# A Mamba-2 scan and a low-rank mixer in one kernel: fills from a repeated column of ones, and a longer fill before the first C B^T

## The chip, the cores and the metric

The kernel runs on one core of a Trainium2 chip. The metric is the device time of one execution in microseconds; lower is better. The engines named below are TensorE (matmul; PE in the profile, its weight loads PEld), VectorE (DVE), ScalarE (ACT), GpSimd (POOL) and SyncE (SP), which issues every load and store.

## The reference

Two blocks follow one another. The first is a chunked state-space scan over x (4 batches, 8 heads, 768 steps, 32 channels) with decays `a` and matrices B and C of 16 columns; the second is a mixer with a low-rank product over the sequence and a two-layer network over the channels.

```python
for c in range(nc):                       # chunks of 32 steps
    cum = np.cumsum(log_a[:, :, sl], axis=-1)
    L = np.exp(cum[:, :, :, None] - cum[:, :, None, :]) * causal
    M = np.einsum('bhin,bhjn->bhij', Cc, Bc) * L
    y_intra = np.einsum('bhij,bhjd->bhid', M, xc)
    y_inter = np.einsum('bhin,bhnd->bhid', Cc, state) * np.exp(cum)[:, :, :, None]
    y[:, :, sl] = y_intra + y_inter
    state = decay_full * state + (decay_from_j * Bc, xc summed over j)
# y as (4, 768, 256)
h = y.transpose(0, 2, 1) @ U @ V
u = y + h.transpose(0, 2, 1)
out = u + np.maximum(u @ w_ch1, 0.0) @ w_ch2
```

## The kernel before

The scan is done in 12 pairs of 128-step blocks (3 pairs for each of 4 batches). For a pair k the steps are: `Q` or `P` scales pieces of B and C by the decays on VectorE (tile `BC`); `V` or `T` transposes them on TensorE (L480) and copies them out (tiles `T` and `Cm`); `g` forms C B^T (L511); `m` and `M` mask it on VectorE; `s` and `u` form and carry the state (L543); `n` and `i`, `j` form the output inside and between chunks (L635, L613); `y` copies it out, `t` turns it. The mixer's steps (`p`, `q`, `a`, `S`, `f`, `e`, `h`, `d`, `U`) follow batch by batch; their matmuls are those of L725, and they make most of the time.

The order of all work is written out by hand. `LOADS` names the first loads; `PLAN` is a string of words, each a step with its indices, and every engine gets its instructions in the order in which `follow` (L859) meets the words. The words `b`, `x`, `w`, `W`, `Z`, `z` issue loads, all on SyncE's queue. The plan begins (L37):

```python
'x1.1 F2.0 A0 Q0.1 x1.0 Q0.0 b2.2 A1 F2.1 Q0.2 V0.1.1 V0.0.0 K0 F1.3 Q1.2 Q1.1 g0 m0 Q1.0 s0 '
```

The word `F` calls `warm` (L320), which calls `idle` (L133): a **fill**, a matmul into a PSUM bank whose result nobody reads. `F2.1` is a fill of two times 128 columns into a bank of tag `x`; the second index chooses among the tags `w`, `x`, `z`, `y`. Two more fills stand in the code ahead of the plan: `warm(3, "x")` (L325), the first work of TensorE, and `warm(1, "x")` (L331), behind the transposes of the decays (L330). Each fp32 matmul is two weight loads and two matmul instructions in the trace. A fill takes `ident` as weights, and `ident` once, two or three times side by side as moving operand.

Before the plan VectorE and GpSimd make the constants. VectorE begins with `ones` (L291) and `ref` (L306); GpSimd makes `ident` (by `make_identity`, L289) and then the triangles `upto` and `low` out of `ones`. `ident` is also what the transposes need. The decays: `a_sb` is loaded (L171), transposed (L330), clipped on VectorE, put through the logarithm on ScalarE (L336); `A0` and `A1` (L366, L370) make the factors `F` of it, `K0` (L381, L384) the carried decays. Between `K0` and `g0` stands the fill `F1.3`; `g0` needs the tiles `Cm`, whose last part ScalarE writes (L490).

VectorE's instructions all show L159 in the profile, the line of a helper; they are told apart by their tiles. Loads show L185, fills L138.

Of the kernel before, what the change touches and what calls it, by code (L numbers as in the profile page):

```python
# [10 lines left out]
FP32 = mybir.dt.float32  # L11
# [22 lines left out]
LOADS = (  # L34
    'b0.0 b0.1 b0.2 x0.0 x0.1 b1.0 b1.1 b1.2 ')
PLAN = (
# [40 lines left out]
def kernel(  # L77
# [27 lines left out]
    nc = tc.nc  # L105
    P = 128
# [17 lines left out]
    const = ctx.enter_context(tc.tile_pool(name="const", bufs=1))  # L124
# [8 lines left out]
    def idle(t, n):  # L133

        while n > 0:
            m = min(n, max(t.shape[1] // P, 1), 4)
            w = min(P, t.shape[1])
            nc.tensor.matmul(out=t[:, :m * w].rearrange("p (m i) -> p m i", i=w), lhsT=ident,  # L138
                             rhs=ident[:, None, :w].to_broadcast([P, m, w]), start=True, stop=True)
            n -= m  # L140

    def bank(tag, *dims):
# [5 lines left out]
    class Kept:  # L148
# [15 lines left out]
    vector = Kept(nc.vector)  # L164
# [7 lines left out]
        out=a_sb,  # L172
# [112 lines left out]
    for word in LOADS.split():  # L285
        loads[word[0]](*(int(v) for v in word[1:].split(".")))

    ident = const.tile([P, P], FP32)
    make_identity(nc, ident)  # L289
    ones = const.tile([P, P], FP32)  # L290
# [29 lines left out]
    def warm(n, tag="w"):  # L320

        idle(bank(tag, 4 * P), n)
# [6 lines left out]
    for g in range(2):  # L329
# [3 lines left out]
        out=la.rearrange("p b c h -> p b h c"),  # L333
# [575 lines left out]
```

## Time and profile before

| what | value |
|---|---|
| median of 3 runs | 226.42 us (226.41, 226.42, 228.46) |
| span of the profiled execution, first to last instruction | 224.7 us |
| its own time around the span | not given by the page |
| TensorE busy | 216.0 us (96%) |
| VectorE, ScalarE, GpSimd busy | 156.7, 114.3, 14.3 us |
| DMA | 14.56 MB in 69518 packets, 63792 of them under 512 bytes |
| first fill | starts at 1.43 us |
| fill ahead of the first C B^T | starts at 8.53 us, lasts 0.38 us |
| first C B^T | starts at 9.56 us |

Times in rows of the profile count from the first instruction. A row of the timeline is: start, duration, engine, line, operation, the tile written and those read, the shape, the count, and in brackets how long the engine stood idle before it and what ended that. A row of a table of stretches is: the stretch, its length, the busy time of each engine with the number of instructions, the clock granted to TensorE, the mean busy share of the DMA engines, GB/s. In a group of instructions the number behind the busy time is the mean duration of one in nanoseconds.

### The profile page before, as it was taken

Reading aid. Unit: us, or ns where it says so; the run is one execution under the profiler, and the core shown is the slowest. Engines: PE = TensorE matmul, PEld = TensorE weight load, DVE = VectorE, ACT = ScalarE, POOL = GpSimd, SP = SyncE. Lnnn points to the kernel's source line nnn. Section 1 sums busy time; section 2 is a strip of 40 time slices with the busy share of each in tenths; the row PEclk is TensorE's granted clock in tenths of the full one; section 3 lists DMA queues with packets and bytes.
Section 4 is the critical chain, followed back from the end, with each engine's and each line's share of the span. In section 5 each row is a group of like instructions: output and inputs, shape, how many; then the busy total and the mean of one; then the engine's idle time right before and its main releaser. Section 6 shows DMA issues by size and latency. Waiting matters only on the chain.

```text
span 224.7 us, 7010 instructions
## 1 busy us (share of the span) xinstructions
PE 216.0 (96%) x3012; PEld 182.8 (81%) x3012; DVE 156.7 (70%) x329; ACT 114.3 (51%) x261; POOL 14.3 (6%) x37
## 2 busy tenths in 40 slices
PE   7888989999999999999999999999999999999993
PEld 4656655656668898987999898887998999999993
DVE  4776878899998866969717785758437964764921
ACT  3334946856994346334453632475237545655410
POOL 3021010012100000202101000100000000000000
PEclk9999999999999999999999999999999999999999
DMA  6997799788645203600002602000020000100011
GB/s 88 127 111 144 132 130 287 139 163 230 92 65 72 51 23 59 84 23 26 3 26 48 96 0 73 3 3 3 1 71 1 0 0 26 47 0 28 32 38 47
DMA packets 69518, 14.56 MB, mean 65 GB/s; under 512 B 63792, under 2 KB 67696, under 8 KB 69488
## 3 DMA queue, kind: packets, MB, share of 16 engines
q1 hardware_dynamic: 69488, 14.13, 34.6%
q8 instruction: 23, 0.38, 0.7%
q14 instruction: 7, 0.06, 0.1%
HBM read 10.98 MB, written 3.15 MB: 63 GB/s over the span
## 4 chain that ended last, share of the span: by engine, by line
PE 91%; DVE 2%; DMA 2%; SPq 1%; issue 1%; POOL 0%; ACT 0%; POOLq 0%; DVEq 0%
PE x L725 31%; PE z L725 24%; PE y L725 12%; PE y L613 4%; PE y L635 3%; PE w L480 3%; PE x L511 3%; PE w L656 2%; DMA bc<-in_B_dram 2%; PE w L543 2%; PE z L511 2%; PE x L138 1%; SPq L185 1%; PE w L679 1%; PE w L138 1%
## 5 line engine op out<-in xcount | busy, mean ns | idle before, releaser
L159 DVE SCALAR_TENSOR_TENSOR words<-words 128x768 fp32r<-128x768 f32 (+6 forms) x44 | 34.6, 806 | 1.9 <-ACT words L416 0.6
L725 PE MATMUL z<-u,w 128*128 128x384 f32 x144 | 34.0, 350 | 0.0
L725 PE MATMUL x<-u,w 128*128 128x384 f32 x144 | 33.1, 348 | 0.0
L730 ACT ACTIVATE x<-x 128x384 f32<-128x384 f32 (+1 forms) x30 | 13.6, 452 | 25.3 <-PE x L725 25.1
L725 PEld LDWEIGHTS z<-u,w 128*128 128x128 f32 x144 | 24.5, 188 | 1.3 <-DVE words L159 0.2
L725 PEld LDWEIGHTS x<-u,w 128*128 128x128 f32 x144 | 24.0, 188 | 1.3 <-ACT x L730 0.6
L159 DVE SCALAR_TENSOR_TENSOR words<-x,words 128x384 fp32r<-128x384 f32 x24 | 13.2, 555 | 16.4 <-ACT words L759 13.7
L725 PE MATMUL x<-w2c,words 128*128 128x256 f32 x112 | 22.5, 338 | 0.0
L730 ACT ACTIVATE z<-z 128x384 f32<-128x384 f32 (+1 forms) x27 | 12.5, 463 | 14.1 <-PE z L725 13.6
L725 PEld LDWEIGHTS x<-w2c,words 128*128 128x128 f32 x112 | 18.2, 189 | 1.3
L725 PE MATMUL y<-w,words 128*128 128x256 f32 x144 | 19.1, 282 | 0.0
L725 PEld LDWEIGHTS y<-w,words 128*128 128x128 f32 x144 | 18.5, 188 | 0.3 <-DVE ytok L159 0.3
L159 DVE SCALAR_TENSOR_TENSOR words<-z,words 128x384 fp32r<-128x384 f32 x24 | 13.2, 551 | 5.7 <-ACT words L759 5.7
L759 ACT ACTIVATE words<-x 128x384 fp32r<-128x384 f32 x24 | 11.6, 490 | 6.3 <-PE x L725 6.1
L759 ACT ACTIVATE words<-z 128x384 fp32r<-128x384 f32 x24 | 11.6, 491 | 4.9 <-PE z L725 4.8
L648 ACT COPY yT<-y 128x256 f32<-128x256 f32 x24 | 7.8, 384 | 10.9 <-PE y L613 10.7
L569 POOL TENSOR_TENSOR Sm<-S,own 128x256 f32<-128x256 f32 (+1 forms) x12 | 7.7, 644 | 87.5 <-DVE S L159 58.1
L159 DVE SCALAR_TENSOR_TENSOR S<-S,kept,w 128x64 f32<-128x64 f32 x40 | 11.2, 280 | 2.7 <-PE w L543 0.9
L613 PE MATMUL y<-T,Sm 32*64 32x64 f32 x352 | 12.4, 239 | 0.4 <-POOL Sm L569 0.3
L725 PE MATMUL x<-w,words 128*128 128x256 f32 x96 | 12.6, 282 | 0.0
L725 PEld LDWEIGHTS x<-w,words 128*128 128x128 f32 x96 | 12.0, 188 | 0.1
L511 PE MATMUL x<-Cm,T 32*64 32x128 f32 x192 | 11.0, 307 | 1.0 <-ACT Cm L490 0.7
(152 smaller groups left out, 400.5 us busy)
## 6 DMA issues: line engine op xcount, KB each, us to landing
words<-in_moe_w_ch_dram SPq DMA_DIRECT2D x7, 512.0 KB, 6.1
x<-in_x_dram SPq DMA_DIRECT2D x24, 128.0 KB, 3.7
out_dram<-ytok SPq DMA_DIRECT2D x24, 128.0 KB, 1.7
bc<-in_B_dram SPq DMA_DIRECT2D x24, 64.0 KB, 3.7
bc<-in_C_dram SPq DMA_DIRECT2D x12, 128.0 KB, 3.8
words<-in_moe_w_ch_dram SPq DMA_DIRECT2D x2, 256.0 KB, 4.5
words<-in_moe_V_dram SPq DMA_DIRECT2D x4, 48.0 KB, 3.1
words<-in_moe_U_dram SPq DMA_DIRECT2D x1, 192.0 KB, 3.5
```

Source lines behind the costliest of these rows:

```text
L138: nc.tensor.matmul(out=t[:, :m * w].rearrange("p (m i) -> p m i", i=w), lhsT=ident, rhs=ident[:, None, :w].to_broadcast([P, m, w]), start= ...
L159: self.last = call(*args, **kwargs)
L480: nc.tensor.transpose(out=tp[:, i, v], in_=s["BC"][:, i, c + v].rearrange("p h n -> p (h n)"), identity=ident)
L511: nc.tensor.matmul(out=g[r][cols, c], lhsT=s["T"][rows, 0, c, cols], rhs=s["Cm"][rows, :, :, ts(2 * c + p, Q)].rearrange("r v t i -> r v i ...
L543: nc.tensor.matmul(out=s["A"][p][ts(r, Q), v], lhsT=s["BC"][half, 0, v, 2 * r:2 * r + 2].rearrange("p h n -> p (h n)"), rhs=x_sb[k][half, ...
L569: nc.gpsimd.tensor_tensor(out=s["Sm"][:, sl], in0=s["S"][:, sl].rearrange("p i (s d) -> p i s d", s=2), in1=own2[:, b, 4 * q + sl.start:4 ...
L613: product = nc.tensor.matmul(out=y[p][ts(r % 2, H), r // 2, c], lhsT=own[ts(r, Q)], rhs=s["T"][ts(r, Q), 1, :, ts(2 * c + p, Q)].rearrange ...
L635: product = nc.tensor.matmul(out=y[p][ts(i, Q), n, c], lhsT=x_sb[k][half, c, h], rhs=s["M"][half, h // 2, c, h % 2], start=fresh(k, p, [i] ...
L648: nc.scalar.copy(out=yp[:, :, :, p], in_=st[k]["y"][p])
L725: nc.tensor.matmul(out=t, lhsT=lhsT, rhs=rhs, start=start, stop=True, skip_group_check=True)
L730: nc.scalar.activation(t, t, AF.Copy, scale=1.0 + EPS)
L759: nc.scalar.activation(gs[j, m // 2][0][:, m % 2], t, AF.Relu, scale=NEAR)
```

## The change

A tile `one` of one column is added and set to 1.0 on VectorE, ahead of `make_identity` and of `ones`. The fills read it in place of `ident`: the weights are that column repeated 128 times, the moving operand is that column repeated over all columns of the fill. In the plan `F1.3` becomes `F3.3`: the fill between `K0` and `g0` has 384 columns in place of 128, in the same bank.

```diff
-    ... A1 F2.1 Q0.2 V0.1.1 V0.0.0 K0 F1.3 Q1.2 Q1.1 g0 m0 Q1.0 s0 '
+    ... A1 F2.1 Q0.2 V0.1.1 V0.0.0 K0 F3.3 Q1.2 Q1.1 g0 m0 Q1.0 s0 '
@@ def idle(t, n):
-            nc.tensor.matmul(out=t[:, :m * w].rearrange("p (m i) -> p m i", i=w), lhsT=ident,
-                             rhs=ident[:, None, :w].to_broadcast([P, m, w]), start=True, stop=True)
+            nc.tensor.matmul(out=t[:, :m * w].rearrange("p (m i) -> p m i", i=w), 
+                             lhsT=one.to_broadcast([P, P]),
+                             rhs=one[:, None, :].to_broadcast([P, m, w]), start=True, stop=True)
@@
+    one = const.tile([P, 1], FP32)
+    vector.memset(one, 1.0)
     ident = const.tile([P, P], FP32)
     make_identity(nc, ident)
     ones = const.tile([P, P], FP32)
```

2 rows, old and new, of the table PLAN are left out of this document.

## The prediction

> **What bounds the kernel now.** I read the page's first two parts, then a table by stretches, then the waits of VectorE and TensorE in the first 33 us, because every edit lies there. The page first (busy shares; the span in 40 slices of 5.6 us):
>
> ```profile
> span 224.7 us, 7010 instructions
> PE 216.0 (96%) x3012; PEld 182.8 (81%) x3012; DVE 156.7 (70%) x329; ACT 114.3 (51%) x261; POOL 14.3 (6%) x37
> PE   7888989999999999999999999999999999999993
> DMA  6997799788645203600002602000020000100011
> ```
>
> TensorE is the bound of the whole, but the first six slices show it mostly at 70 to 90% beside DMA engines that are 60 to 90% busy. The table by stretches says it sharper (columns: stretch: length, busy PE, PEld, DVE, ACT, POOL, PEclk, DMA share, GB/s):
>
> ```profile
> 0.00:10.00 10.00, 7.92 (x56) 5.49 (x64) 5.13 (x20) 3.67 (x9) 2.06 (x12) 1.00 0.85 106
> 10.00:21.00 11.00, 9.95 (x374) 6.71 (x358) 7.73 (x26) 3.84 (x14) 2.01 (x5) 1.00 1.04 126
> 21.00:33.00 12.00, 10.49 (x307) 6.99 (x308) 9.75 (x30) 8.28 (x23) 1.49 (x4) 1.00 0.87 129
> 33.00:60.00 27.00, 26.62 (x419) 16.31 (x425) 24.77 (x57) 19.60 (x43) 2.68 (x4) 1.00 0.82 187
> 60.00:225.00 165.00, 161.05 (x1890) 147.34 (x1881) 109.35 (x200) 78.87 (x176) 6.07 (x12) 1.00 0.16 34
> ```
>
> Up to 33 us the DMA engines are as good as full (shares 0.85, 1.04, 0.87) and TensorE idles 2.08, 1.05 and 1.51 us; from there on it idles 0.38 us in 27 and 3.95 in 165. So the time is the moment at which the DMA-fed start hands over to TensorE, plus some 192 us that no edit touches. Which wait ends last in the start? The timeline's rows for VectorE and TensorE carry it in brackets (idle before, and what ended it):
>
> ```profile
> 6.14 1.02 DVE L159 TENSOR_TENSOR BC<-bc,F 128x128 f32<-128x128 f32 x3 [1.44 <-DMA bc<-in_B_dram]
> ...
> 20.21 0.69 DVE L159 TENSOR_TENSOR BC<-bc,F 128x512 f32<-128x512 f32 x1 [1.26 <-DMA bc<-in_C_dram]
> ```
>
> ```profile
> 21.55 0.63 PE L480 MATMUL w<-ident,BC 128*128 128x128 f32 x4 [0.67 <-DVE S L159]
> ...
> 32.65 0.66 PE L480 MATMUL w<-ident,BC 128*128 128x128 f32 x4 [0.40 <-DVE BC L159]
> ```
>
> VectorE stands idle until a piece of B or C has landed, and TensorE stands behind it at 21.55 (through the `S` that VectorE makes after 20.21) and at 32.65. The chain that ended last shows the second joint, where a landing of B is followed (over VectorE) by TensorE, which holds the chain from there:
>
> ```profile
> 28.00 3.78 DMA bc<-in_B_dram
> ...
> 32.65 0.66 PE w L480 x4
> ```
>
> What TensorE gains before 21.55 is given back at these joints as longer idle time; what it loses is paid only beyond 0.67 us at 21.55, and again beyond 0.40 us at 32.65. The landings themselves should not move: SyncE issues its loads one behind the other from 0.81 us on, and the first of them that takes over a buffer in use is this one, after 24 us:
>
> ```profile
> 0.81 0.38 SPq L171 DMA_DIRECT2D a_sb<-in_a_dram  x1
> ...
> 24.17 1.28 SPq L185 DMA_DIRECT2D x<-in_x_dram  x1
> ```
>
> **Part one: the column of ones.** The timeline's rows by engine: VectorE's first memset and, for its price, the memset of one column for `bias`; GpSimd's `ident`, and `upto` behind it; then TensorE:
>
> ```profile
> 0.90 0.17 DVE L159 MEMSET ones<- 128x128 f32 x1 [0.90 <-PEq L893]
> ...
> 4.34 0.06 DVE L159 MEMSET bias<- 128x1 f32 x1
> ```
>
> ```profile
> 1.08 0.29 POOL masks.py:199 TENSOR_SCALAR_AFFINE_SELECT ident<-ident 128x128 f32<-128x128 f32 x1
> 1.33 0.29 POOL L294 TENSOR_SCALAR_AFFINE_SELECT upto<-ones 128x128 f32<-128x128 f32 x1
> ```
>
> ```profile
> 1.43 1.65 PE L138 MATMUL x<-ident 128*128 128x384 f32 x2 [1.43 <-POOL ident masks.py:199]
> ...
> 2.88 0.29 PEld L330 LDWEIGHTS w<-ident,a_sb 96*128 96x128 f32 x2 [0.95 <-DMA a_sb<-in_a_dram]
> ```
>
> Added: one memset of 0.06 us, ahead of `ones` on VectorE. It would run 0.90 to 0.96; with the 0.06 us that lay between the end of `ident` (1.08 + 0.29 = 1.37) and the first fill (1.43), the fill starts at about 1.02, **0.41 us sooner**. `ones` and what follows it move back by 0.06 us or less; `upto`, which reads `ones`, starts at 1.33 behind `ident` on POOL while `ones` ends at 1.07, so 0.2 us of cover remains. The first work that counts, the transposes of `a_sb`, waits for its DMA until 2.88 in either kernel. The fill ahead of them then ends at 1.02 + 1.65 = 2.67 instead of 3.08: the gain becomes idle time in front of 2.88. One wait is added: those transposes are now the first to need `ident`; it has been done since 1.37, so this costs at most one extra wait instruction, a few hundredths, and is covered by the VectorE wait that ends at 6.14. Worth: **0**.
>
> The later fills keep their number, their place and, but for one, their columns. No row here has a matmul whose operands repeat one column. Bounds: not quicker than the 128-column step below; if reading it were twice as slow, the fills of 384 and 256 columns that follow C B^T (0.82 and 0.60 us by the rows of part two; F2.1 and F3.0 before the first joint, F2.3 before the second) would each cost as much again: 0.60 + 0.82 - 0.67 = 0.75 us passes the first joint, 0.75 + 0.60 - 0.40 = 0.95 us the second, 227.4. I take no difference: in the trace the fills' moving operand already is a repeated block, and their times follow the number of columns alone.
>
> **Part two: 384 columns for 128.** First the fill itself and a later one of 256 columns (for the price of columns), then what C B^T waits for:
>
> ```profile
> 8.53 0.38 PE L138 MATMUL y<-ident 128*128 128x128 f32 x2
> ...
> 12.74 0.60 PE L138 MATMUL x<-ident 128*128 128x256 f32 x2
> ```
>
> ```profile
> 8.87 0.64 ACT L490 ACTIVATE Cm<-w,slot 128x128 f32<-128x128 f32 x2
> ...
> 9.56 0.13 PEld L511 LDWEIGHTS x<-Cm,T 32*64 32x64 f32 x2 [0.85 <-ACT Cm L490]
> ```
>
> A fill of 128 columns takes 0.38 us, one of 256 takes 0.60: 0.22 us per 128 columns, so 384 take 0.82. It starts at 8.53 and ends at 9.35. The first C B^T (L511) waits until 9.56 for the second `Cm` of ScalarE, which ends at 8.87 + 0.64 = 9.51. The 0.44 us added lie wholly in TensorE's idle time and leave 0.21 us over. Worth: **0**. Were the clock still at half there, the fill would last as the first one does, 1.65 us, to 10.18, and C B^T would be 0.62 us late; that stays just under the 0.67 us at 21.55.
>
> **The clock.** The fills are there to bring it up, and the page's PEclk row reads 9 from the start, so durations must tell:
>
> ```profile
> L138 PE MATMUL x<-ident 128*128 128x128 f32 x2 | 0.7, 448 | 0.0
> ```
>
> ```profile
> L480 PE MATMUL w<-ident,BC 128*128 128x128 f32 x4 | 0.6, 272 | 0.0
> ```
>
> The same shape takes 448 ns a matmul in the window to 4 us and 272 in that from 7: the speed about doubles in between, at about 7.2 us by the L480 rows. Three stretches of the table give what hangs on it:
>
> ```profile
> 3.40:7.20 3.80, 3.80 (x17) 2.53 (x17) 2.10 (x10) 1.05 (x3) 0.15 (x1) 1.00 1.16 133
> 7.20:10.60 3.40, 2.75 (x76) 2.31 (x75) 2.44 (x7) 1.41 (x5) 0.44 (x1) 1.00 1.09 130
> 7.20:14.00 6.80, 5.72 (x179) 4.05 (x177) 5.32 (x17) 3.21 (x11) 1.08 (x2) 1.00 1.26 107
> ```
>
> The change shifts when TensorE becomes busy by 0.41 us and puts up to 0.2 us of new idle time (2.67 to 2.88) in front of the transposes. A rise that came sooner would shorten TensorE's work from 3.4 to 7.2 us, 3.80 us of busy time, by half at most, 1.9 us; of this nothing passes the landing at 6.14 and the 1.26 us of idle VectorE at 20.21. [...]
>
> **The sum**, against the profiled execution: 224.7 + 0 + 0 = 224.7 us of span. The page gives no other time of that execution; the median shown, 226.42, lies 1.7 us above its span, and I carry this over: **226.4 us**. Two of the three runs shown are at 226.41 and 226.42, the third at 228.46.
>
> **Rivals.** *Sooner clock without cover* (0.05): the clock rises a step sooner and the DMA joints do not absorb it, as they would fail to if SyncE's stalls in the start depended on TensorE. For it: the chain of waits begins on TensorE, with the first fills, before the DMAs take it over. Against: the 1.26 us at 20.21. It gives up to 1.9 and 0.41 us less: 224.1 to 225.7.
>
> *The new idle time spoils a step of the clock* (0.15): fills that end before `a_sb` has landed leave TensorE idle where it was busy, and the rise comes later, about one stretch of the table later. Half clock from 7.2 to 10.6 doubles 2.75 us of work, of which 0.65 us goes into idle time and 0.67 + 0.40 into the joints: at most 1.0 us more, 226.5 to 227.4. Against it: 0.2 us of idle time is less than the 1.4 us that TensorE idles before the first fill now.
>
> *Repeated ones do not hold the clock up* (0.10), the one that ends **slower**: the fills would be no activity to whatever grants the clock, and it would rise only on real work. Its place is the stretch from 7.2 us on, and it decides from a rise at about 14 us: 5.72 us of work doubled, less 1.08 of idle time and 1.07 of joints, is 3.6 us more, 230.0; with a rise at 10.6 it is the case above. For it: no row shows such operands. Against: `ident` too is nearly all zeros, and the clock did rise on it. [...]
>
> *It does not do what it says*: the first fill is held to 1.4 us by something else than `ident`. That gives 226.4 too and is in the main case.
>
> **The numbers.** No change 0.70, a spoiled step 0.15, slow on ones 0.10, faster 0.05. The range takes the first two, with the double-priced fills and the third run's 228.46 as the reason to reach further up than down: 225.7 to 228.0. A hundredth, 2.3 us, is about what a measurement of this kernel can tell from no change. Only the low end of the first rival passes it downward (0.04, with a little for what I do not see), most of the third upward (0.11); the rest, 0.85, is within.
>
> **What would show it.** First fill at about 1.0 on a wait for VectorE; transposes of `a_sb` still at 2.88; the fill before C B^T about 0.8 us long and C B^T still at about 9.56; VectorE's wait at 20.2 and TensorE's at 32.65 where they were. Wrong, if the 448 ns shape is still seen after 8 us, if the fills take longer per column than 0.22 us in 128, or if the B piece that landed at 31.8 lands earlier or later.

## The result, and the profile after

The changed kernel takes **225.04 us** (median of 22 executions) against 226.46 for the kernel before (22): a ratio of **0.9931, 95% interval 0.9908 to 0.9953**. That is 0.7% faster: within the 1% called no change, but below the range that was given. Executions of either kernel in which the granted clock falls for one stretch (last section) are some 2 us longer; rows are compared with profiles that lack it unless the text says so.

The page of the changed kernel (span, busy shares, the 40 slices, the loads' queue with packets, MB and share of the 16 DMA engines):

```profile
span 223.3 us, 7012 instructions
PE 215.1 (96%) x3012; PEld 181.6 (81%) x3012; DVE 156.7 (70%) x330; ACT 114.5 (51%) x261; POOL 14.7 (7%) x37
...
PE   7989799999999999999999999999999999999993
...
DMA  6987599777737014300003402000020000100111
...
q1 hardware_dynamic: 69488, 14.13, 31.8%
```

and the last of these lines on the page of the kernel before:

```profile
q1 hardware_dynamic: 69488, 14.13, 34.6%
```

The span is 1.4 us shorter. The same packets and the same bytes took less of the DMA engines: 34.6% of 224.7 us is 77.7 us an engine, 31.8% of 223.3 is 71.0. Nothing in the change is a load. The page of DMA issues for the first 33 us alone says where (queue: packets, MB, share; then the loads of B: count, KB, median us from issue to landing), before and after:

```profile
q1 hardware_dynamic: 28892, 3.89, 91.2%
...
bc<-in_B_dram SPq DMA_DIRECT2D x12, 64.0 KB, 4.2
```

```profile
q1 hardware_dynamic: 29064, 4.22, 78.9%
...
bc<-in_B_dram SPq DMA_DIRECT2D x12, 64.0 KB, 3.3
```

More bytes in less DMA time: 7.74 us of full engines per MB before (0.912 x 33 / 3.89), 6.17 after. A load of B lands 0.9 us sooner behind its issue. The timeline of VectorE after, to be held against 6.14, 20.21 and the BC ahead of 32.65:

```profile
0.88 0.06 DVE L160 MEMSET one<- 128x1 f32 x1 [0.88 <-PEq L896]
...
5.95 0.94 DVE L160 TENSOR_TENSOR BC<-bc,F 128x128 f32<-128x128 f32 x3 [1.16 <-ACT F L376]
...
19.03 0.69 DVE L160 TENSOR_TENSOR BC<-bc,F 128x512 f32<-128x512 f32 x1 [0.99 <-issue]
...
30.70 0.68 DVE L160 TENSOR_TENSOR BC<-bc,F 128x512 f32<-128x512 f32 x1
```

The wait for `bc` is gone ahead of 5.95 and of 30.70. Ahead of 19.03 VectorE still stands for 0.99 us. The row puts that down to `issue`, but a piece of B issued at 14.78 lands 4.2 us later, at 18.98; the same piece before, issued at 15.48, landed 4.6 us later, at 20.08, just ahead of 20.21. So the wait for a landing is still there and ends 1.2 us sooner. TensorE's timeline after (L483 and L514 are L480 and L511 of before):

```profile
0.99 1.65 PE L138 MATMUL x<-one 128*128 128x384 f32 x2 [0.99 <-DVE one L160]
...
3.00 0.55 PE L333 MATMUL w<-ident,a_sb 96*128 96x96 f32 x2 [0.36 <-DMA a_sb<-in_a_dram]
...
8.20 0.81 PE L138 MATMUL y<-one 128*128 128x384 f32 x2
9.24 0.34 PE L514 MATMUL x<-Cm,T 32*64 32x128 f32 x2 [0.23 <-ACT Cm L493]
...
20.45 0.66 PE L483 MATMUL w<-ident,BC 128*128 128x128 f32 x4
...
23.61 0.45 PE L638 MATMUL y<-M,x 64*32 64x64 f32 x28 [1.01 <-issue]
...
31.44 0.66 PE L483 MATMUL w<-ident,BC 128*128 128x128 f32 x4
...
39.55 0.63 PE L483 MATMUL w<-ident,BC 128*128 128x128 f32 x4 [0.15 <-PE z L514]
...
219.37 0.28 PE L728 MATMUL y<-ps,Vs 128*128 128x256 f32 x1
```

TensorE has no wait left at either joint (21.55 and 32.65 of before are 20.45 and 31.44), and the two later rows have these partners before:

```profile
40.85 0.63 PE L480 MATMUL w<-ident,BC 128*128 128x128 f32 x4 [0.15 <-PE z L511]
...
220.86 0.28 PE L725 MATMUL y<-ps,Vs 128*128 128x256 f32 x1
```

So 1.30 us are won by 40 us, and 1.49 at the last matmul. Following the same matmul through both traces (its start before, and how much later it starts after):

```
before      3.26   9.75  18.63  20.43  23.75  28.27  39.12  53.67 108.38 140.77 220.86
after      +0.09  -0.33  -0.91  -0.36  +0.08  -0.12  -1.30  -1.30  -1.30  -1.36  -1.49
```

What TensorE had gained was given back by 23.75, though not where the prediction put it: TensorE passes the first joint 1.10 us sooner and then stands for 1.01 us ahead of 23.61. The profile shows nothing that it waits for there (`issue`); the kernel with nothing but an unread tile, below, has the same wait of 1.02 us at 24.46. The lasting gain appears between 28 and 39 us, around the second joint. What moved there is SyncE's issue of the three pieces of B that feed it, before and after:

```profile
28.00 1.91 SPq L185 DMA_DIRECT2D bc<-in_B_dram  x3
```

```profile
26.77 1.85 SPq L186 DMA_DIRECT2D bc<-in_B_dram  x3
```

They are issued 1.23 us sooner, and the first of them lands 2.7 us behind its issue, at about 29.4, in place of 3.78 us, at 31.78. At the piece of B ahead of them, issued at 23.67 before and at 23.65 after, the two queues are level; the 1.23 us arise in the two issues between, that of `x` (1.28 us before, 0.53 after) and that of C (2.45 and 1.99). Why a column of ones makes B land sooner is what the experiments had to find.

### The profile page after: what moved, and what is told of

The parts are those of the page before. It is cut to its first block, busy times and chain, and to the rows that moved or that the text cites. A ratio compares the mean times of both kernels' runs of the same rounds, so it can differ in the third digit from the quotient of the medians.

```text
span 223.3 us, 7012 instructions
## 1 busy us (share of the span) xinstructions
PE 215.1 (96%) x3012; PEld 181.6 (81%) x3012; DVE 156.7 (70%) x330; ACT 114.5 (51%) x261; POOL 14.7 (7%) x37
## 3 DMA queue, kind: packets, MB, share of 16 engines
q1 hardware_dynamic: 69488, 14.13, 31.8%
## 4 chain that ended last, share of the span: by engine, by line
PE 90%; DVE 4%; issue 2%; ACT 1%; DMA 1%; POOL 0%; DVEq 0%; POOLq 0%; ACTq 0%
PE x L728 31%; PE z L728 24%; PE y L728 12%; PE y L616 4%; PE y L638 4%; PE x L514 3%; PE w L483 3%; PE w L659 2%; PE w L546 2%; PE z L514 2%; PE w L682 1%; DMA a_sb<-in_a_dram 1%; DVE words L160 1%; PE w L138 1%; DVE S L160 1%
## 5 line engine op out<-in xcount | busy, mean ns | idle before, releaser
L160 DVE SCALAR_TENSOR_TENSOR words<-words 128x768 fp32r<-128x768 f32 (+6 forms) x44 | 34.6, 806 | 1.9 <-ACT words L419 0.6
L733 ACT ACTIVATE x<-x 128x384 f32<-128x384 f32 (+1 forms) x30 | 13.6, 452 | 25.1 <-PE x L728 24.1
L638 PE MATMUL y<-M,x 64*32 64x64 f32 x768 | 11.0, 224 | 1.1 <-issue 1.0
```

The lines of the kernel that those rows point to most:

```text
L160: self.last = call(*args, **kwargs)
L638: product = nc.tensor.matmul(out=y[p][ts(i, Q), n, c], lhsT=x_sb[k][half, c, h], rhs=s["M"][half, h // 2, c, h % 2], start=fresh(k, p, [i] ...
L733: nc.scalar.activation(t, t, AF.Copy, scale=1.0 + EPS)
```

## The experiments

Ratios are to the kernel before run beside each; 12 executions each, 6 for two of them. "Long packets" are packets of 64 or 128 bytes (the rows of B, C and x) that took over 60 ns in the first 50 us of the profiled execution. Such a packet usually takes 11 or 13 ns; before has 130 long ones, up to 1031 ns, and after has none.

**The parts of the change.** Part one alone, with `F1.3` kept:

> Only the column of ones; the fill ahead of the first C B^T keeps 128 columns. The whole change measured 0.993 of the kernel before (225.0 against 226.5 us). If the earlier start of the first fill (0.99 us in place of 1.43) is what pays, because it brings the speed of TensorE up sooner: 0.993 again, about 225.0. If the longer fill is what pays: 1.000. If both pay by half: 0.9965.

Measured 0.9967 [0.9936, 0.9998], no long packet: near the figure for two parts that pay by half, which the next run contradicts. In 4 of its 12 executions the clock fell (last section), in none of the 12 of the changed kernel run beside it. Part two alone, with `ident`:

```diff
-    ... V0.0.0 K0 F1.3 Q1.2 ...
+    ... V0.0.0 K0 F3.3 Q1.2 ...
```

> Only the fill of 384 columns ahead of the first C B^T; all fills read the identity, the first still starts at about 1.43 us. If the start pays: 1.000, about 226.4. If the longer fill pays: 0.993, about 225.0, and fewer runs that lie 1.5 to 2 us above the others (8 of 22 runs of the kernel before did).

Measured 1.0028 [0.9989, 1.0066], 107 long packets. Its timeline of TensorE has the longer fill, and C B^T still waiting behind it for ScalarE's `Cm`:

```profile
8.71 0.81 PE L138 MATMUL y<-ident 128*128 128x384 f32 x2
9.76 0.35 PE L511 MATMUL x<-Cm,T 32*64 32x128 f32 x2 [0.23 <-ACT Cm L490]
```

The length is worth nothing. Is it then the sooner start? The whole change, with the column made out of `ident`, so that the fills start late:

```diff
     one = const.tile([P, 1], FP32)
-    vector.memset(one, 1.0)
...
+    vector.tensor_scalar(out=one, in0=ident[:, :1], scalar1=0.0, scalar2=1.0,
+                            op0=ALU.mult, op1=ALU.add)
```

> The whole change, but the column of ones is derived on VectorE from the finished identity (times 0, plus 1), so the first fill starts at about 1.5 us as in the kernel before or a little later. If the start pays: 1.000, about 226.4. If the operand itself pays (one repeated element read in place of a 128 by 128 tile): 0.993, about 225.0. If the longer fill pays: 0.993 as well, and then the run with the longer fill alone tells the two apart.

```profile
1.62 1.65 PE L138 MATMUL x<-one 128*128 128x384 f32 x2 [1.62 <-DVE one L160]
```

The first fill starts 0.19 us later than before the change, and the kernel is as fast as the changed one: 0.9939 [0.9914, 0.9965], no long packet. (One of its 12 executions took 506.11 us; nothing here shows why, and the ratio leaves it out.) The changed kernel beside it:

> The changed kernel itself, as a yardstick beside the other three on the same chip: 0.993 (0.991 to 0.995) if the measured gain is the change's. About 1.000 if the gain hung on the runs in which it was first measured.

Measured 0.9926 [0.9894, 0.9958]. So neither the start nor the length makes the gain. What is left of part one is its operand, and the tile that holds it.

**The tile.** In the built program `one` takes 32 bytes a partition ahead of `ident`, and every tile behind it lies 32 bytes further: the first `bc` tile at 71872 in place of 71840, `x` at 80064 for 80032, `words` at 88256 for 88224. The kernel before with nothing but an unread tile there, and no instruction for it:

```diff
+    gap = const.tile([P, 1], FP32)
     ident = const.tile([P, P], FP32)
```

> The kernel before, with one unread tile of one column allocated ahead of the identity. It adds no instruction; every tile allocated after it starts 32 bytes higher, so the landing places of the B, C and x loads are multiples of 64 bytes (71872) and no longer 32 beyond one (71840). If the place of the tiles is what pays: about 225.0 us, 0.994 to 0.997, no small DMA packet over 60 ns in the first 20 us (the kernel before has 93 of them, up to 1031 ns), landings 1 us or more sooner from 9 us on. If the operand of the fills pays: 1.000, about 226.4.

Measured **0.9920 [0.9888, 0.9952]**, no long packet: the whole gain, with nothing of the change in it. Its first 33 us:

```profile
q1 hardware_dynamic: 29089, 4.28, 80.0%
```

0.80 x 33 / 4.28 = 6.17 us per MB, the figure of the changed kernel. With the longer fill added:

> As the run with the gap alone, and the fill ahead of the first C B^T has 384 columns; all fills read the identity. If place and length make up the change: 0.993, as the whole change. If repeated ones are needed for the longer fill to pay: as the gap alone, or worse by the share of runs in which the clock granted to TensorE falls for a while (6 of 12 with the longer fill of the identity in the old places, none of 12 in the whole change).

Measured 0.9898 [0.9835, 0.9962] over 6 executions, no long packet. The other way round, all of the change but the tile, with `one = ones[:, :1]`, a column that was there already:

> The whole change without its tile: the fills read the first column of the tile of ones that is there already, 384 columns ahead of C B^T, and all tiles stay in the old places (71840). If the place pays: 1.000, about 226.2, with small packets up to 1 us again. If the operand pays: 0.993.

Measured **1.0019 [0.9976, 1.0062]**, 151 long packets, and for the first 33 us 0.87 x 33 / 3.67 = 7.82 us per MB:

```profile
q1 hardware_dynamic: 28744, 3.67, 87.0%
```

And the whole change with a second tile of one column behind `one`, which moves all the rest by 64 bytes:

> The whole change with one more unread tile of one column behind its own, so that B, C and x land 32 bytes beyond a multiple of 64 again (71904), with no other difference. If the place pays: 1.000, about 226.2, long small packets again. If the operand pays: 0.993, about 224.9.

Measured 1.0024 [0.9989, 1.0060], 139 long packets. The change with its tile's place taken away is worth nothing, and the place without the change is worth all of it.

**Which tiles.** Only `bc` moved by 32 bytes; `x` and all behind it by 64:

```diff
@@ def load_x(k, blocks=(0, 1)):
+        if not x_sb:
+            raw.tile([P, 1], FP32, tag="gap", name="gap", bufs=1)
@@
+    gap = const.tile([P, 1], FP32)
     ident = const.tile([P, P], FP32)
```

> The kernel before with one unread column ahead of the identity and another ahead of the x tiles: only the four B and C tiles start at multiples of 64 bytes; x, the weight words and all working tiles stay 32 beyond one. If the B and C loads (rows of 64 and 128 bytes) are what the place helps: about 225.0, 0.992 to 0.995. If the x loads (rows of 128 bytes) count as well: in between, 0.996 to 0.998, with long packets of 128 bytes left. If it is not the loads but the engines' working tiles: 1.000.

Measured 0.9968 [0.9946, 0.9990], no long packet. The gap in `load_x` alone, so that `bc` stays and `x`, `words` and the engines' working tiles move by 32:

> The kernel before with one unread column behind the B and C tiles: these stay 32 bytes beyond a multiple of 64, x, the weight words and all working tiles are on one. If the B and C loads are it: 1.000, about 226.3, long packets of 64 bytes left at 11 us. If x counts too: 0.996 to 0.998. If the working tiles are it: 0.992.

Measured 1.0004 [0.9961, 1.0047], 124 long packets. Only the working tiles moved by 32 (a gap in the pool behind the loads' tiles):

```diff
+    att.tile([P, 1], FP32, tag="gap", name="gap", bufs=1)
```

> The kernel before with one unread column behind all load tiles: B, C, x and the weight words stay 32 bytes beyond a multiple of 64, only the engines' working tiles are on one. If the landing places of the loads are what counts: 1.000, about 226.3, long small packets as before. If the working tiles count: 0.992.

Measured 0.9994 [0.9954, 1.0035], 167 long packets. Long packets come and go with the place of `bc` alone. (The engines' constants ahead of `bc` moved with it in every such kernel, but their readers take as long as before between 8 and 33 us: the updates of `S` 280 ns, the transposes into `x` 297.) For the first 33 us, `bc` moved and then working tiles moved:

```profile
q1 hardware_dynamic: 28780, 3.66, 74.5%
```

```profile
q1 hardware_dynamic: 28784, 3.67, 87.4%
```

6.72 and 7.86 us per MB.

**Which places.** My theory was now that a multiple of 64 bytes is what `bc` needs. Gaps of 24, 40, 72 and 56 columns (96, 160, 288 and 224 bytes) in place of the one column, the one column again, and the change with 64 bytes behind `one` (the place of the gap of 96):

> The kernel before with a gap of 96 bytes in place of 32: B, C, x and the weight words start at multiples of 256 bytes (71936), not only of 64 (71872). If 64 is what counts: as the gap of 32, 0.992, about 225.0. If larger multiples help further, as rows of 128 bytes and more could use: 0.985 to 0.990, and the fastest of all.

Measured 0.9989 [0.9955, 1.0023], no long packet.

> The kernel before with the unread column of 32 bytes again, beside a gap of 96 and of 160 on one chip. 0.992 as before, about 225.0, if the first result holds; 0.996 or more if it was a lucky one.

Measured 0.9892 [0.9842, 0.9942] over 6 executions, no long packet.

> The gap of 96 bytes again (loads land on multiples of 256). If every multiple of 64 is as good: the same as the gap of 32 within 0.3%. If starting at a multiple of 256 costs part of the gain: 0.997 to 0.999 once more, 1 us slower than the gap of 32.

Measured 0.9964 [0.9919, 1.0009], no long packet.

> A gap of 160 bytes: loads land 64 beyond a multiple of 256. If every multiple of 64 is as good: the same as the gaps of 32 and 96. If only the multiple of 256 is worse: 0.992, as the gap of 32.

Measured 0.9962 [0.9919, 1.0006], with **17 long packets**, up to 252 ns.

> The whole change with 64 bytes more ahead of the identity, so that its tiles lie where the gap of 96 puts them. If every multiple of 64 is as good: 0.993, as the change itself. If the multiple of 256 costs: 0.997 to 0.999. If the fills of the change add something of their own: faster than the gap of 96 by that.

Measured 0.9963 [0.9923, 1.0003], no long packet.

> The kernel before with an unread tile of 72 columns (288 bytes) ahead of the constants: everything behind it moves by 256 bytes more than with a tile of one column. The loads of B and C start on a multiple of 64 again, and with the same remainder (192) against 256 as with the one column. If the remainder against 256 sets what a place is worth, the ratio is that of the one column, 0.989 to 0.992, and no packet of 64 or 128 bytes lasts over 60 ns. If any multiple of 64 gives the same and the one column's lead is chance or something else of that one place, the ratio is 0.996 to 0.999, as with 96 and 160 bytes. If the place has nothing to do with it, 1.00 and some 110 to 160 long packets.

Measured 0.9910 [0.9868, 0.9953], no long packet.

> The same with 56 columns (224 bytes): the loads start on a multiple of 64, at 128 against 256, the one remainder that no run has had. If the remainder sets the worth, this may lie anywhere from 0.989 to 0.999 while the 288 bytes beside it give 0.989 to 0.992; if any multiple of 64 gives the same, both give the same ratio. No packet of 64 or 128 bytes over 60 ns in either case; with them, 1.00.

Measured 0.9940 [0.9903, 0.9978], no long packet.

The 17 long packets at 160 bytes speak against the theory: `bc` lies on a multiple of 64 there. A tile of `bc` holds, in each stretch of 256 bytes, one row of B's first piece (`b.0`, 64 bytes), one of its second (`b.2`, 64 bytes) and one of C (`b.1`, 128 bytes). So at each place it is always the same piece whose rows cross a multiple of 256:

```
bc moved by  start mod 256  rows that cross  long packets in (transfers in order of issue)
0 (before)   160            b.2              x0 28 (behind b0.2), x1 14 (behind b1.2), b3.0 42 (behind b2.2), b5.2 22 (behind b4.2), b5.0 11 (behind b5.2)
64 (e8)      224            b.0              C0 10, C1 32, C2 41 (each behind b.0), b2.0 24 (behind b3.0), x4 22 (behind b4.0); x0, x1 none
160 (e15)    64             b.1 (C)          b1.2 4, b3.2 11 (each behind b.1), x2 2 (behind b2.1)
32, 288      192            none             none
96           0              none             none
224 (e18)    128            none             none
```

(The packets were counted in groups of 1024 by their order of start, 1024 being one transfer; neighbours on the queue overlap somewhat, and the table names the largest groups. The last two of before lie at 30.2 to 31.3 us, in the second joint.) The stalled transfer changes with the place, and it is the one queued **right behind** the transfer whose rows cross. Had a start off a multiple of 64 been the cause, 0 and 64 bytes would show the same transfers, since all rows start off one in both, and 160 bytes none. That it is 256 and not 128 is shown for the rows of C: at 192 they are cut at a multiple of 128, with no long packet, and at 64 at one of 256, with 17. No run cuts rows of B at a multiple of 128 alone. B's rows, cut into 32 and 32 bytes, come with 130 and 139 long packets (before and at 64 bytes); C's, cut into 64 and 64, with 17. Rows of `x` cross too, half of them after the change and half in the kernel with only `bc` moved, and nothing stalls behind them; why not is open. What is cut here is the place written to, and the long packets are those of the next transfer; why that one pays is not shown. Of the places without crossing rows, 0, 128 and 192 have no long packet and 433.4, 435.0 and 433.5 us of packet time over the first 50 us.

**Why 32 and 288 bytes do better than 96, 160 and 224.** On the same chip the six executions with 32 bytes reach 225.18 at most, and the twelve with 96 bytes start at 225.18; the medians with 288 and 224 are 225.05 and 225.87. The traces, followed as above, put this behind 108 us, where `words` is an operand of the mixer's matmuls. By how much the last matmul gains or loses after 108 us against the profile before, by the place of `words`:

```
words mod 256   160            192                                              224            0                  64      128
moved by        0              32, in the last 288                              64             96                 160     224
us              0.00,-0.02,    -0.19,-0.42,-0.62,-0.34,-0.66,-0.60,-0.41,-0.45,  +0.20,+0.09   +0.35,+0.37,+0.35  -0.18   +0.58
                +0.18          -0.34
```

The -0.45 is the kernel whose `bc` stayed; with only the working tiles moved it was +0.18, so it goes with `words` or `x`, which moved by the same bytes in every run. The rows below read `words`. The groups behind 108 us (busy us, mean ns) for before, the gap of 32, that of 96, and the kernels with `x` and `words` moved and with only the working tiles moved:

```profile
L725 PE MATMUL x<-w,words 128*128 128x256 f32 x96 | 12.6, 282 | 0.0
```

```profile
L726 PE MATMUL x<-w,words 128*128 128x256 f32 x96 | 12.2, 278 | 0.0
```

```profile
L726 PE MATMUL x<-w,words 128*128 128x256 f32 x96 | 12.7, 283 | 0.0
```

```profile
L727 PE MATMUL x<-w,words 128*128 128x256 f32 x96 | 12.3, 279 | 0.0
```

```profile
L726 PE MATMUL x<-w,words 128*128 128x256 f32 x96 | 12.6, 282 | 0.0
```

A matmul of this group takes 278 to 281 ns with `words` at 192 (281 in the changed kernel itself, which gains least there), 282 at 160 and 224, 281 at 64, and 283 at 0 and 128; with its fellows that write `y` and `z` there are 288. So a place has two prices. One falls before 40 us, by the rows of B: the ratio of the kernel with only `bc` moved puts it at 0.7 us, 0.2 to 1.2 by its interval. The other falls behind 108 us, most likely by `words`: 0.3 to 1.0 us between the mean of the best place and those of the others. 32 and 288 bytes have both gains, and the change happens to use the place of 32. The first price scatters: the shift at 108 us is -0.46 to -1.58 in the ten single profiles with `bc` free of crossing and neither a moved clock nor `x` placed apart, +0.06 in the kernel with only `bc` moved, -0.23, -0.23, -0.44 and -1.08 in four with crossing rows of B, and -0.83 in the one with crossing rows of C. SyncE's issue of the three pieces of B scatters as well: 25.1 to 28.4 us in the 13 profiles without crossing rows, 25.8 to 28.2 in the six with crossing rows of B. One profile proves little here; the ratios carry it. They show that the place of `bc` sets the long packets and costs time; the path from there to an earlier hand-over is read from one pair of profiles and is not shown. Why the mixer's matmuls are faster with `words` at 192 is open, and no version is clearly faster than the change: the intervals of the gaps of 32 and 288 bytes overlap its own.

## Why the prediction was wrong

**What failed is the sentence "The landings themselves should not move"**, and with it the first words of the cost of part one, "Added: one memset of 0.06 us". The tile brought an instruction, 0.06 us, and a place. The prediction priced the instruction and never asked where the tile lies and what it moves; the new place took 81.7 us of packet time (516.6 to 434.9 over the 64- and 128-byte packets of the first 50 us, 5.1 us for each of 16 engines) out of the start, and the last of its own conditions, "if the B piece that landed at 31.8 lands earlier or later", came true: it landed at about 29.4. VectorE's wait at 20.2 and TensorE's at 32.65, which were to stay, moved to 19.03 and 31.44. The reason given for still landings was that the loads wait for no engine before 24 us; that said nothing of how long their packets take. (The first load into a buffer in use is also not the `x` at 24.17 but the piece of B at 23.67: `b4.0` is the fifth tile of four buffers.) In this pair of profiles the missing term is -1.3 us at the hand-over and -0.2 behind 108 us; 226.4 less these is 224.9, and 225.04 was measured.

**The frame was right in the main.** The time is set where the DMA-fed start hands over to TensorE: 1.30 of the 1.49 us are won there and stay to the end. Gains of TensorE before that were given back (-0.91 at 18.63, +0.08 at 23.75), but in the wait at 23.61, not at the joint at 21.55. Not every later microsecond was out of reach of the edit either: 0.19 us were won behind 108 us.

**Part one, worth 0: right.** The first fill started at 0.99 on VectorE, forecast 1.02; the transposes of `a_sb` at 3.00, forecast 2.88; the extra wait and the difference of one execution from another can account for it (the unread tile alone, without the wait, gave 2.96, 0.04 less). A start at 1.62 lost nothing (0.9939). The operand costs nothing: the 128-column shape takes 448 ns before and after, and with the ones but not the place the ratio is 1.0019.

**Part two, worth 0: right.** The fill of 384 columns took 0.81 us, forecast 0.82, and C B^T waited behind it for `Cm`, 0.23 us for the forecast 0.21. It ran at 9.24 instead of 9.56; by the clock's record in the traces the clock had risen at 5.39 us in this execution and at 7.17 in that of before.

**The rivals.** *Sooner clock without cover* gave 224.1 to 225.7, which holds the time, for the wrong reason: the clock does rise sooner in this profile, and TensorE's gain from it is gone by 23.75. Across the profiles the rise lies between 4.6 and 8.7 us and goes with no part of the change. *The new idle time spoils a step* fell for this change: the clock rose sooner in its profile, not a stretch later. Over all profiles a small cost is not excluded: the five whose first fill starts at 0.99 have the rise at 5.4 to 8.7 us, the others at 4.6 to 7.6. That a late rise is late by a whole stretch of 3.4 us, from 7.2 to 10.6, was the author's assumption; no run shows it, and the latest rise seen is at 8.7. *Repeated ones do not hold the clock up* fell: in the profiles whose fills read repeated ones the clock rose at 4.6 to 8.7 us, in the kernel that reads `ones` at 4.6, and not at 14. *It does not do what it says* fell by the first fill's row.

**The chances.** The 0.85 on within 1% came true, by luck: 0.70 of it stood on no change, and only 0.05 on faster, by another cause. The range was too narrow below, since the one cause that could pass the joints downward, sooner landings, was taken to be out of reach.

## What to carry to other kernels

When an edit adds, drops or resizes a tile, write down the addresses of the tiles behind it before costing anything else: rows of loads that cross a multiple of 256 bytes (some 0.7 us) and operands of the matmuls that bind (0.3 to 1.0 us, most likely by `words`) were worth more here than the edit, which without its place gave 1.0019. To tell the two apart, run the old kernel with an unread tile of the same size, and the new one with the size taken back. A change that every argument prices at nothing and that still moves the time by the better part of a per cent has most likely moved something else.

## What was not expected of the hardware

**A load stalled the one behind it.** With rows of 64 bytes cut by a multiple of 256, packets of the next transfer in the queue lasted up to 1031 ns in place of 11 or 13; with rows of 128 bytes cut in half, 17 packets were long, up to 252 ns. The mechanism inside the DMA engines was not seen.

**The clock falls in the middle.** In 58 of 151 executions of the kernel before the mean granted clock was 0.982 to 0.993, and their median is 229.06 us against 226.17 for the others. With crossing rows under another edit it was 23 of 60, at the places of 96, 160 and 224 bytes 16 of 60, and at those of 32 and 288, with the change or with a gap, 11 of 72; that a start which feeds TensorE better meets it less often is a reading of these counts, and it adds to the ratios. Among the executions of one chip that lack it the medians are 226.19 us before (22 executions), 225.20 with only `bc` placed (11), 225.70 with `x`, `words` and the working tiles placed (7) and 226.31 with the working tiles alone (8): some 1.0 us by `bc` and 0.5 by `x` or `words`. The kernel that reads `ones` shows it in its profile: the page's clock row, and two stretches (length, busy PE, PEld, DVE, ACT, POOL, granted clock, DMA share, GB/s):

```profile
PEclk9999996999999999999999999999999999999999
```

```profile
31.90:35.30 3.40, 1.49 (x19) 1.23 (x20) 1.46 (x4) 1.34 (x4) 0.00 (x0) 1.00 0.79 192
35.40:38.70 3.30, 3.30 (x8) 1.69 (x7) 3.27 (x9) 1.59 (x5) 0.00 (x0) 0.50 1.10 332
```

TensorE is busy 1.49 of 3.40 us (44%) at the second joint, and in the 3.3 us from 35.40 on the granted clock is 0.50. By the clock's record in the traces the rise and the fall lie 30.7 us apart in this profile, nine times 3.41 us, about the length of the fall, and eight times 3.41 us in the two of the gap of 96 bytes, which have the fall too. Counted in steps of 3.41 us from each profile's rise, TensorE was busy for 45% (the stretch above, placed by the record), 58 and 60% of the step ahead of the three falls, and for 65% or more of every step before 45 us that no fall followed (the least in the changed kernel: 2.22 us of the 3.41 from 22.46 on). These are three falls; that the idle time brings them on is not shown.
